# The score mask of an attention step is cut where its maximum is cut: three heads' mask and maximum, then the fourth head's

## The chip, the core and the metric

The kernel runs on one core of a Trainium2 chip. The metric is the time of one execution on the device, in microseconds; the time of a kernel is the median of several runs. The engines are named as in the profile: PE (TensorE matmul), PEld (TensorE weight load, which overlaps with PE), DVE (VectorE), ACT (ScalarE), POOL (GpSimd), SP (SyncE).

## What is computed

A transformer block of one sequence of 2048 tokens, 640 wide: a modulated layer norm, attention of 32 heads (20 wide) in a sliding window of 256 tokens, a residual, a second modulated layer norm and an MLP (1536 wide, tanh GELU). Cut to the attention:

```python
qkv = (x @ wqkv).reshape(B, S, 3, H, Dh)          # H = 32, Dh = 20, W = 256
scores = einsum("bhqd,bhkd->bhqk", q, k) * Dh ** -0.5
mask = (idx[:, None] - idx[None, :] >= 0) & (idx[:, None] - idx[None, :] < W)
scores = where(mask, scores, -1e9)
p = softmax(scores, axis=-1)
o = einsum("bhqk,bhkd->bhqd", p, v)
```

## The kernel before

All matmuls run in fp32 or split a factor into a high and a low part. The program has three parts in time: a prologue to about 50 us (layer norm, first projections), attention with the projections laid between, to about 540 us, and the output projection and the MLP after that, which run on PE almost without a gap.

**The attention steps.** The heads are taken four at a time (a quad), the tokens in two halves, and a half in eight blocks of 128 queries. That makes 2 x 8 x 8 = 128 items, one per step t of the loop near the end of the function. A step t works on two items at once. The first is the scores item t (the tile s): queries against the three blocks of 128 keys in the window, for four heads. Only the maximum of each row is wanted from it, and goes into the tile nm. The second is the item t - 11 (LAG), the tile e: the same scores once more, turned round and with the maximum already subtracted through two more rows of the operands. It goes through the exponential into the tile pt, and two steps later (PVLAG) pt is multiplied with v into the tile o.

**What a step issues, in order.** On PE `score_batch` issues the e and the s matmuls as one mixed batch; then come the o matmuls (`pv_stage`), then a share of the projection's matmuls (tile pp), set by tables of numbers (EXTRA, LEAST, and so on). On DVE: the mask of e (`e_mask`), the mask of s and the maximum (`s_max`), then whatever the plan has put into this step: layer norm statistics, residues of projections, sums of the modulation. On ACT the exponential, on POOL the rest of the masking of pt. The engines' queues keep this program order (class `Ordered`).

**The s tile and its banks.** From step 11 to 127 the four heads of s lie side by side, 384 columns each, in one fixed tile that is used anew in every step (`score_banks`). It has three PSUM banks of 512 columns: head slot 0 lies in bank 0, slot 1 in banks 0 and 1, slot 2 in banks 1 and 2, slot 3 in bank 2. A matmul that would cross a bank is cut there (`cuts`). The order of the pieces in the mixed batch is the table BOTH: three of e, then slot 1's piece in bank 1, slot 1's piece in bank 0, slot 3 (bank 2), and so on. In a few batches two of these change places. So slot 3 is mostly the third s matmul of a batch, and it is the first to touch bank 2.

**The maximum in two pieces.** In 84 of the steps from 11 on the maximum is taken in two instructions: slots 0 to 2 (CUT = 3), which lie in banks 0, 1 and 2, then slot 3, in bank 2. In 33 steps, those of the table WHOLE, one instruction takes all four. Every maximum is kept in the list `maxima` with the banks that it reads. In the next step `score_batch` tells the scheduler that a matmul does not depend on a maximum of other banks. So the matmuls in banks 0 and 1 may start after the first maximum, and those in bank 2 after the second.

**The mask of s.** Of the three key blocks only two need a maximum: the oldest block's columns that are inside the window are copied over the masked-out columns of the newest block. That is `copy_predicated` on the last 128 columns of each head, with the first 128 as data (or a large negative constant, negc, where the oldest block does not exist). Before the change this is one instruction for all four heads, 128x512, ahead of both maxima.

All engine calls go through the helper `go` of `OrderedEngine`, so in the profile each stands at line 116, and the tiles' names tell them apart.

Of the kernel before, what the change touches and what calls it, by code (L numbers as in the profile page):

```python
# [17 lines left out]
P = 128  # L18
# [103 lines left out]
def block_kernel(ctx: ExitStack, tc: tile.TileContext, x, wqkv, wo, w1, b1, w2, b2, c, crow, wmod, wcol, sel, outT):  # L122
    core = tc.nc
    nc = Ordered(tc)
# [30 lines left out]
    negc = const.tile([P, 1, 1], F32, name="negc")  # L155
    nc.vector.memset(negc, NEG)
    mask_t = const.tile([P, 3, P], F32, name="mask_t")
    masks = {}
# [375 lines left out]
    fixed, maxima = {}, []  # L534
# [11 lines left out]
    def width():  # L546
        return 384 if LAG <= now[0] < 2 * NQB * QUADS else 512
# [65 lines left out]

    def s_max(it, s, c0):

        data = negc.to_broadcast([P, 4, P]) if c0 else s[:, :, 0:P]
        nc.vector.copy_predicated(s[:, :, 2 * P : 384], masks["s"].to_broadcast([P, 4, P]), data)
        del maxima[:]
        n = width()
        for lo, hi in ((0, CUT), (CUT, 4)) if n == 384 and now[0] not in WHOLE else ((0, 4),):  # L620
            red = nc.vector.tensor_reduce(
                it["quad"]["nm"][:, lo:hi, it["key"][2]], s[:, lo:hi, max(c0, P) : 384], AX.X, ALU.max
            )
            if n == 384:
                maxima.append((red.ins, range(lo * n // 512, (hi * n - 1) // 512 + 1)))

    def m_rows(it):
        half, quad, _, _ = it["key"]
# [515 lines left out]
    def lay_units(room):  # L1144
        used, act = collections.Counter(), collections.Counter()
        for t in asides:
            used[t] += 0.5
        t, turns, where = 0, {}, []
        for i, (key, c2) in enumerate(seq):
            fast = i < FAST  # L1150
            acc = (lambda i=i: pools["o"].tile([P, CHUNK], F32, tag="o", name=f"ppo{i}")) if fast and i % 2 else None
            mms, ev = unit(*key, c2, nc.vector if i in LOV else gp, acc)
            if key[0] and 2 + c2 in turns:
                t = max(t, turns[2 + c2] + 1)
            t0, left = t, list(mms)
            pieces = []
            while left:
                have = room * (t + 1 - FAST) - sum(used[j] for j in range(FAST, t + 1))
                n = len(left) if fast else min(len(left), max(LEAST, int(have + 0.5) + EXTRA.get(t, 0)))
                if len(left) - n < 3 and n < MOST:  # L1160
                    n = len(left)
                pieces.append((t, left[:n]))
                used[t] += n
                left = left[n:]
                t += 1
            where.append((i, key, c2, pieces, ev))
            if key[1] == 2:
                used[t] += V_COST
            if not key[0] and not [1 for k, c in seq[i + 1 :] if not k[0] and c == c2]:

                at = max(t, turns[2] + 5) if c2 else t
                for kt in range(KT):
                    used[at + kt] += X_COST
                turns[2 + c2] = at + KT + (1 if c2 else 2)
        return t, where, turns

    lo, hi = 4.0, 16.0
    for _ in range(30):
        room = (lo + hi) / 2
        lo, hi = (lo, room) if lay_units(room)[0] <= LAST else (room, hi)  # L1180
    _, where, turns = lay_units(hi)
    ready_w = [(seq[0][0], 0)]
    for i, key, c2, pieces, ev in where:
        t0, t1 = pieces[0][0], pieces[-1][0]
        for t, mms in pieces:
            cut = max(len(mms) - 3, 3)
# [73 lines left out]
    for (mms, (copy, turn)), lo, hi in zip(units, LATE_AT[3::2], LATE_AT[4::2]):  # L1260
        spread(plan, [step(1, go) for go in mms], lo, hi)
        hi = max(hi, TOMID + 0.5)
# [38 lines left out]
    n = len(s_items)  # L1301
# [6 lines left out]
    for t in range(n + LAG + PVLAG + 4):  # L1308
# [31 lines left out]
        if si:  # L1340
            s_max(si, *got)
# [47 lines left out]
    for ch in range(nch):  # L1389
        yhi, ylo = ([y[:, kt] for kt in range(KT)] for y in yT[ch % 2])  # L1390
        ts = slice(ch * CHUNK, (ch + 1) * CHUNK)
        lo, hi = (LO0, 9) if ch == 0 else (4 * ch + 5, 4 * ch + 9)
# [100 lines left out]
```

## Time and profile before

| | us |
|---|---|
| median of 3 runs | 977.62 |
| lowest and highest run | 977.16, 978.79 |
| the profiled execution | 978.3 |
| its span in the profile | 976.6 |
| granted clock of TensorE, mean | 0.998 |

The span goes from the first to the last instruction of the profiled execution. The rows of the profile read: engine, operation, output tile <- input tiles, shape, number; then busy time and mean duration in ns; then the engine's idle time just ahead of them and what ended it. Rows of the timeline read: start in us, duration in us, engine, line, operation; neighbouring instructions of one kind stand in one row, with the number behind x and the shape of the first. Rows of the waits read: who waited, for whom, us in total, number of times, the longest. Rows of windows read: stretch, its length, busy time of PE, PEld, DVE, ACT and POOL, the granted clock, the share of the DMA engines, GB/s.

### The profile page before, as it was taken

The numbers are of one execution on the slowest core, as the hardware profiler recorded it, in microseconds if no ns is written. First come the engines' busy times: TensorE is split into PE (matmuls) and PEld (weight loads), VectorE is DVE, ScalarE is ACT, GpSimd is POOL, SyncE is SP. The second block draws the span as 40 slices with busy tenths as digits, with TensorE's granted clock in tenths as the row PEclk, the third lists the DMA queues.
The fourth block names the chain that finished last, engine by engine and source line by source line (L and its number), as shares of the span: only waits on it lengthen the run. The fifth ranks groups of instructions, "written<-read, shape, count | busy, mean of one in ns | idle before, by whom it ended". The sixth has DMA issues, their size and how long they took to land.

```text
span 976.6 us, 20093 instructions
## 1 busy us (share of the span) xinstructions
PE 947.7 (97%) x7789; PEld 752.6 (77%) x7789; DVE 592.9 (61%) x999; ACT 442.4 (45%) x777; POOL 485.8 (50%) x673
## 2 busy tenths in 40 slices
PE   8899999999999999999898999999999999999998
PEld 8677777777777777777677787888888888888886
DVE  6564977978776786767888556563534444342112
ACT  3724555666644545555545654434333243333222
POOL 4423555677864364553646844654554454332121
PEclk9999999999999999999999999999999999999999
DMA  8366778756778459854852245444423342114113
GB/s 307 99 207 199 243 226 260 224 170 168 220 231 236 121 174 283 241 155 120 224 161 76 81 137 161 127 130 138 138 57 103 115 144 85 54 57 145 54 43 119
DMA packets 98974, 152.17 MB, mean 156 GB/s; under 512 B 8864, under 2 KB 42112, under 8 KB 98880
## 3 DMA queue, kind: packets, MB, share of 16 engines
q1 hardware_dynamic: 89664, 142.50, 48.2%
q10 hardware_dynamic: 9216, 8.39, 2.7%
q8 instruction: 62, 1.02, 0.4%
q14 instruction: 32, 0.26, 0.1%
HBM read 98.51 MB, written 51.58 MB: 154 GB/s over the span
## 4 chain that ended last, share of the span: by engine, by line
PE 82%; DVE 7%; ACT 4%; POOL 2%; DMA 2%; issue 2%; SPq 1%; DVEq 0%; POOLq 0%; ACTq 0%
PE pp L116 17%; PE out L116 16%; PE h L116 16%; PE e L116 8%; PE o L116 7%; PE wo L116 7%; PE s L116 4%; ACT pt L116 3%; DVE e L116 2%; PE ppo L116 2%; DVE nm L116 1%; PE yt L116 1%; PE pv L116 1%; PE xt L116 1%; DMA wc<-in_wcol 1%
## 5 line engine op out<-in xcount | busy, mean ns | idle before, releaser
L116 POOL TENSOR_SCALAR_AFFINE_SELECT pt<-pt 128x512 f32<-128x512 f32 x192 | 127.7, 665 | 131.8 <-ACT pt L116 119.4
L116 ACT ACTIVATE pt<-e 128x1024 f32<-128x1024 f32 (+1 forms) x120 | 133.7, 1115 | 67.2 <-DVE e L116 63.8
L116 DVE TENSOR_REDUCE nm<-s 128x1 f32<-128x256 f32 (+5 forms) x212 | 158.0, 779 | 4.4
L116 POOL TENSOR_TENSOR w2lo<-w2r,w2hi 128x640 fp32r<-128x640 f32 x48 | 78.7, 1639 | 160.2 <-ACT w2hi L116 160.2
L116 DVE CAST ghi<-g 128x512 fp32r<-128x512 f32 x48 | 28.1, 585 | 155.7 <-ACT g L116 155.7
L116 PE MATMUL e<-qbuf,kbuf 62*128 62x128 f32 (+2 forms) x773 | 112.8, 330 | 9.1 <-ACT pt L116 7.6
L116 PEld LDWEIGHTS e<-qbuf,kbuf 62*128 62x128 f32 x773 | 81.2, 186 | 48.5 <-ACT pt L116 23.2
L116 PE MATMUL pp<-hhi,w_hi 128*128 128x512 f32 x265 | 113.4, 428 | 0.2 <-ACT pf L116 0.2
L116 PE MATMUL s<-kbuf,qbuf 60*128 60x384 f32 (+2 forms) x728 | 106.6, 303 | 4.0 <-DVE nm L116 1.6
L116 PE MATMUL pp<-hlo,w_hi 128*128 128x512 f32 x265 | 108.1, 408 | 1.3 <-POOL hlo L116 1.3
L116 DVE COPY_PREDICATED e<-mask_t,e 128x512 f32<-128x512 uint32 x96 | 66.6, 694 | 66.2 <-PE e L116 62.6
L116 PE MATMUL pp<-hhi,w_lo 128*128 128x512 f32 x265 | 106.8, 403 | 0.0
L116 PEld LDWEIGHTS s<-kbuf,qbuf 60*128 60x128 f32 x728 | 89.8, 187 | 14.0 <-DVE nm L116 6.1
L116 PE MATMUL o<-pt,vbuf 128*32 128x128 f32 x2688 | 99.6, 277 | 0.7 <-ACT xT L116 0.7
L116 PE MATMUL out<-ghi,w2hi 128*128 128x512 f32 x240 | 95.5, 398 | 0.5 <-ACT g L116 0.5
L116 PE MATMUL out<-glo,w2hi 128*128 128x512 f32 x240 | 94.0, 391 | 0.0
L116 PE MATMUL out<-ghi,w2lo 128*128 128x512 f32 x240 | 93.9, 391 | 0.0
L116 POOL TENSOR_TENSOR w_lo<-wraw,w_hi 128x128 fp32r<-128x128 f32 x171 | 76.0, 475 | 32.6 <-ACT w_hi L116 32.6
L116 PE MATMUL h<-yhi,w1hi 128*128 128x512 f32 x220 | 87.8, 399 | 0.0
L116 PE MATMUL h<-ylo,w1hi 128*128 128x512 f32 x220 | 86.2, 392 | 0.0
L116 PE MATMUL h<-yhi,w1lo 128*128 128x512 f32 x220 | 86.0, 391 | 0.0
L116 DVE COPY_PREDICATED s<-mask_t,s 128x512 f32<-128x512 uint32 x112 | 77.1, 689 | 11.8 <-PE s L116 11.5
(179 smaller groups left out, 1839.0 us busy)
## 6 DMA issues: line engine op xcount, KB each, us to landing
w2r<-in_w SPq DMA_DIRECT2D x48, 320.0 KB
qbuf<-q_scr SPq DMA_DIRECT2D x60, 240.0 KB
wraw<-in_wqkv SPq DMA_DIRECT2D x36, 320.0 KB
kbuf<-k_scr SPq DMA_DIRECT2D x44, 240.0 KB
q_scr<-stage SPq DMA_DIRECT2D x20, 512.0 KB
k_scr<-stage SPq DMA_DIRECT2D x20, 512.0 KB
o_scr<-oT ACTq DMA_DIRECT2D x64, 128.0 KB
wm<-in_wmod SPq DMA_DIRECT2D x20, 320.0 KB
```

The lines of the kernel that those rows point to most:

```text
L116: return self.tc.keep_in_program_order(op(*args, **kw))
```

## The change

In the 84 steps in which the maximum is taken in two pieces, the mask is too, cut at the same head, and each piece of the mask stands directly ahead of its maximum. In all other steps nothing changes. The pieces of the mask enter the list `maxima` with the banks of their slots, so that the next step's matmuls in banks 0 and 1 do not depend on the fourth head's mask either.

```diff
     def s_max(it, s, c0):
 
-        data = negc.to_broadcast([P, 4, P]) if c0 else s[:, :, 0:P]
-        nc.vector.copy_predicated(s[:, :, 2 * P : 384], masks["s"].to_broadcast([P, 4, P]), data)
         del maxima[:]
         n = width()
         for lo, hi in ((0, CUT), (CUT, 4)) if n == 384 and now[0] not in WHOLE else ((0, 4),):
+            data = negc.to_broadcast([P, hi - lo, P]) if c0 else s[:, lo:hi, 0:P]
+            cut = nc.vector.copy_predicated(
+                s[:, lo:hi, 2 * P : 384], masks["s"].to_broadcast([P, hi - lo, P]), data
+            )
             red = nc.vector.tensor_reduce(
                 it["quad"]["nm"][:, lo:hi, it["key"][2]], s[:, lo:hi, max(c0, P) : 384], AX.X, ALU.max
             )
             if n == 384:
-                maxima.append((red.ins, range(lo * n // 512, (hi * n - 1) // 512 + 1)))
+                banks = range(lo * n // 512, (hi * n - 1) // 512 + 1)
+                maxima.extend((op.ins, banks) for op in (cut, red))
```

How the instructions stand on DVE in step 94 (the one that the prediction follows in the timeline), before, with what each waits for; e is the tile of the turned scores, s the scores, nm the maxima:

```order
L116 COPY_PREDICATED e_2_3_5439<-mask_t,e_2_3_5439 128x4x128 [waits PE_49,Activation_49]
L116 COPY_PREDICATED s_1_3_995<-mask_t,s_1_3_995 128x4x128 [waits DVE_49,PE_49]
L116 TENSOR_REDUCE nm_3_5105<-s_1_3_995 128x3 [waits DVE_49]
L116 TENSOR_REDUCE nm_3_5105<-s_1_3_995 128x1
L116 COPY_PREDICATED e_2_4_5490<-mask_t,e_2_4_5490 128x4x128 [waits PE_49,Activation_49]
```

and in the changed kernel, the same step on DVE:

```order
L116 COPY_PREDICATED e_2_3_5499<-mask_t,e_2_3_5499 128x4x128 [waits PE_49,Activation_49]
L116 COPY_PREDICATED s_1_3_995<-mask_t,s_1_3_995 128x3x128 [waits DVE_49,PE_49]
L116 TENSOR_REDUCE nm_3_5160<-s_1_3_995 128x3 [waits DVE_49]
L116 COPY_PREDICATED s_1_3_995<-mask_t,s_1_3_995 128x128 [waits DVE_49]
L116 TENSOR_REDUCE nm_3_5160<-s_1_3_995 128x1 [waits DVE_49]
L116 COPY_PREDICATED e_2_4_5551<-mask_t,e_2_4_5551 128x4x128 [waits PE_49,Activation_49]
```

The mask of s has become two instructions, and the second stands between the two maxima. DVE_49 is the semaphore that DVE's own instructions count up. The fourth head's mask waits until the first maximum is done, and the fourth head's maximum until that mask is done; before, the second maximum had no wait of its own. The first mask still waits for the last matmul of the batch that it needs.

On PE the order is the same in both kernels. The batch that follows these maxima, in the changed kernel:

```order
L116 MATMUL e_2_4_5551<-qbuf_100,kbuf_103 128x256 [waits Activation_49]
L116 MATMUL e_2_4_5551<-qbuf_100,kbuf_103 128x384 x2
L116 MATMUL s_1_3_995<-kbuf_104,qbuf_101 128x256 [waits DVE_49]
L116 MATMUL s_1_3_995<-kbuf_104,qbuf_101 128x128
L116 MATMUL s_1_3_995<-kbuf_104,qbuf_101 128x384 [waits DVE_49]
```

The first s matmul (slot 1, bank 1) waits for the maximum of three heads, the third (slot 3, bank 2, 128x384) for the maximum of the fourth. In this kernel as before, each of the two is held only by its own maximum; what moved is what stands ahead of these maxima on DVE. ACT, POOL and the DMA queues have the same rows in both kernels.

## The prediction

> **What bounds the kernel now.** I read the page first (busy times), then the stretch in which attention runs, then the waits of TensorE and VectorE in that stretch, and at last single steps in the timeline.
>
> ```profile
> span 976.6 us, 20093 instructions
> PE 947.7 (97%) x7789; PEld 752.6 (77%) x7789; DVE 592.9 (61%) x999; ACT 442.4 (45%) x777; POOL 485.8 (50%) x673
> ```
> ```profile
> 100.00:540.00 440.00, 426.85 (x4879) 319.53 (x4878) 348.12 (x516) 239.36 (x446) 256.96 (x400) 1.00 0.66 195
> 540.00:977.00 437.00, 429.64 (x2406) 359.49 (x2404) 186.65 (x339) 157.98 (x254) 192.69 (x210) 1.00 0.34 105
> ```
> The two window rows give busy time of PE, PEld, DVE, ACT and POOL, then the granted clock. The change touches only 100 to 540 us, where the score tile is 384 wide. There PE is busy 427 of 440 us and DVE 348: PE sets the pace, but DVE is close behind, and full speed was granted throughout (1.00). A microsecond by which PE is held up there moves the end by as much, since behind it PE is just as full.
>
> Who holds PE up in this stretch:
>
> ```profile
> PEld s L116 <- DVE nm L116: 6.1, 15, 1.2
> ```
> The weight loads of the next scores wait for the maxima (nm), 6.1 us in all. This row counts only idle time; how close the other steps are is seen in one ordinary step (94):
>
> ```profile
> 408.45 0.70 DVE L116 COPY_PREDICATED e<-mask_t,e 128x512 f32<-128x512 uint32 x1 [0.77 <-PE e L116]
> 409.06 0.69 DVE L116 COPY_PREDICATED s<-mask_t,s 128x512 f32<-128x512 uint32 x1
> 409.78 1.29 DVE L116 TENSOR_REDUCE nm<-s 128x3 f32<-128x768 f32 x2
> 411.84 0.70 DVE L116 COPY_PREDICATED e<-mask_t,e 128x512 f32<-128x512 uint32 x1 [0.77 <-PE e L116]
> ```
> ```profile
> 411.12 0.18 PEld L116 LDWEIGHTS s<-kbuf,qbuf 60*128 60x128 f32 x1
> ```
> The two maxima end at 409.78 + 1.29 = 411.07. At 411.12, 0.05 later, the load for the fourth head starts, the one that writes bank 2. What is left of the batch takes until 411.84, where the mask of e starts. So the step is a ring: mask of e, mask of s, two maxima, fourth head on PE, rest of e, mask of e. It takes 3.39 us (411.84 - 408.45), and whatever lengthens DVE's part between the mask of s and the second maximum lengthens it by as much.
>
> Of the 84 steps with two maxima I set the end of the second against the start of the fourth head's load. In 35 the load starts 0.05 us after, as here: it is the second maximum that it waits for. The first and the last of the 35:
>
> ```profile
> 111.04 0.42 DVE L116 TENSOR_REDUCE nm<-s 128x1 f32<-128x256 f32 x1
> ...
> 522.95 0.42 DVE L116 TENSOR_REDUCE nm<-s 128x1 f32<-128x256 f32 x1
> ```
> ```profile
> 111.51 0.18 PEld L116 LDWEIGHTS s<-kbuf,qbuf 60*128 60x128 f32 x1
> ...
> 523.42 0.18 PEld L116 LDWEIGHTS s<-kbuf,qbuf 60*128 60x128 f32 x1
> ```
> In 25 more the load comes less than 0.31 us later than that; their slacks lie between 0.01 and 0.30 us and add up to 3.75 us. The first of these is a maximum that ends at 118.64, with a load 0.24 later, a slack of 0.19:
>
> ```profile
> 118.36 0.28 DVE L116 TENSOR_REDUCE nm<-s 128x1 f32<-128x128 f32 x1
> ```
> ```profile
> 118.88 0.18 PEld L116 LDWEIGHTS s<-kbuf,qbuf 60*128 60x128 f32 x1
> ```
> The last is that of 534.07 (slack 0.26). In the other 24 steps the slack is larger.
>
> **The change, part by part.** PE, ACT, POOL and the DMA queues keep their order; DVE gets 84 instructions more. Durations, from the groups of DVE in the same stretch (mean ns behind the busy time):
>
> ```profile
> L116 DVE TENSOR_REDUCE nm<-s 128x3 f32<-128x768 f32 x81 | 77.7, 959 | 2.8
> L116 DVE COPY_PREDICATED s<-mask_t,s 128x512 f32<-128x512 uint32 x104 | 71.6, 688 | 2.8 <-PE s L116 2.6
> ...
> L116 DVE TENSOR_REDUCE nm<-s 128x4 f32<-128x1024 f32 x30 | 36.8, 1226 | 1.0
> ...
> L116 DVE TENSOR_REDUCE nm<-s 128x1 f32<-128x256 f32 x81 | 33.6, 415 | 0.0
> ...
> L116 DVE COPY_PREDICATED_SCALAR s<-mask_t,negc 128x512 f32 x12 | 8.9, 744 | 0.0
> ```
> *Length of the masks.* From 256 to 1024 columns a maximum grows by (1226 - 415) / 768 = 1.056 ns a column, between 768 and 1024 by 1.04: about 0.133 us for one head's 128 columns, and a fixed part near 0.15. No mask of another width stands in the trace. Three heads' mask is then 0.69 - 0.13 = 0.56; the fourth's is 0.69 - 0.40 = 0.29. Its bounds are 0.13 (columns alone) and 0.69 (width without effect). I take 0.29, since the maximum of the same 128 columns above took 0.28.
>
> *Hand-overs.* In step 94 the mask of s starts 0.09 before the mask of e ends (409.06 against 409.15): its waits were over long before. The first maximum waits for the mask and starts 0.03 after its end (409.78 against 409.75). The second waits for nothing new: the pair takes 1.29 and its parts 0.96 + 0.415, so it starts 0.085 before the first ends. A wait on the instruction just ahead thus costs about 0.12 us. In the new order both the fourth head's mask and its maximum have such a wait.
>
> *The sum for one step,* from the start of the first mask. Before: first maximum ends at 0.72 + 0.96 = 1.68, second at 0.72 + 1.29 = 2.01. After: mask 0.56, maximum from 0.59 to 1.55, mask from 1.58 to 1.87, maximum from 1.90 to 2.32. The first maximum ends 0.13 earlier, the second 0.31 later. I call these 0.31 D. With the bounds of the short mask D is 0.15 to 0.71; the rows near it make that 0.25 to 0.37, down if one of the two waits costs half as much, up by the 0.056 by which the form with a constant (744) exceeds the other (688).
>
> Against one row a rule can be laid: one maximum over four heads takes 1.226, two without a wait between them 1.29, so one more instruction alone costs 0.064. The Trainium skill, in Vector Engine (DVE) Microarchitecture Reference, section 5.2 Measured stream behaviour on trn2, gives about 75 ns per instruction beside 1.0417 ns a column, after queue overlap; the rows agree, and it speaks against splitting. By that alone the 35 steps would lose 2.6 us, an estimate from its figure; I go by the rows with a wait.
>
> *What of it lies on the path.* The earlier end of the first maximum frees banks 0 and 1 sooner, but the fourth head stands third among the s matmuls of the batch, and PE takes its queue in order: what starts sooner waits at the fourth head. I count this gain as nothing. If I am wrong it is 0.13 in each of the 16 steps whose first load of s starts 0.05 after the first maximum's end, 2.1 us; the first and the last of the 16:
>
> ```profile
> 110.17 0.96 DVE L116 TENSOR_REDUCE nm<-s 128x3 f32<-128x768 f32 x1
> ...
> 509.06 0.96 DVE L116 TENSOR_REDUCE nm<-s 128x3 f32<-128x768 f32 x1
> ```
> ```profile
> 111.18 0.18 PEld L116 LDWEIGHTS s<-kbuf,qbuf 60*128 60x128 f32 x1
> ...
> 510.07 0.18 PEld L116 LDWEIGHTS s<-kbuf,qbuf 60*128 60x128 f32 x1
> ```
> The later second maximum costs 35 x 0.31 = 10.9, and 25 x 0.31 - 3.75 = 4.0 in the near ones: 14.9. Counting slack to the start of the matmul and not of its load, since PE often still has a matmul under way, gives 11.7. I take the middle, 13.3.
>
> Behind the waiting instruction on DVE stands the next mask of e or other work. In most steps DVE is idle ahead of that mask:
>
> ```profile
> DVE e L116 <- PE e L116: 68.3, 71, 2.4
> ```
> That cover is missing where statistics or residues fill the gap, as here:
>
> ```profile
> 221.99 1.29 DVE L116 TENSOR_REDUCE nm<-s 128x3 f32<-128x768 f32 x2
> 223.20 0.88 DVE L116 BATCH_NORM_STATS2 st<-xt 128x6 f32<-128x320 f32 x2
> 224.18 0.21 DVE L116 BATCH_NORM_AGGREGATE mv<-st 128x2 f32<-128x12 f32 x1
> 224.30 0.68 DVE L116 COPY_PREDICATED e<-mask_t,e 128x512 f32<-128x512 uint32 x1
> ```
> There the mask of e starts late, with it the exponential and the next e matmuls. This step passes its 0.31 on to the next, and the two behind it have no idle time here either, so nearly 0.9 us gather. For two or three such places I put 2 us (0 to 3), an estimate. Against that, PE's waits for work that does not hang on the mask shrink when PE comes later:
>
> ```profile
> PEld pm L116 <- ACT oT L116: 2.2, 3, 1.4
> PEld e L116 <- ACT w_hi L116: 1.8, 5, 0.4
> PEld e L116 <- ACT oT L116: 1.4, 4, 0.4
> ```
> Of these 5.4 us I take off a quarter, 1.3 (0 to 3). The sum: 13.3 + 2 - 1.3 = **14 us**.
>
> The profiled execution took 978.3 us (span 976.6), 0.7 over the median of the runs, 977.62. So 978.3 becomes 992.3, and the median **991.6**.
>
> **Rivals.**
> 1. *The waits are free.* If handing over costs nothing extra, D falls by 2 x 0.12 to 0.07, and the 35 steps lose 2.5, the near ones 0.2: 980.3. The 0.03 against -0.085 in the step above speaks against it. The Trainium skill has this rule, in VectorE: DVE Perf Modes, section The DRAIN you can't avoid: a semaphore between chained instructions costs nothing extra; here the trace does not agree. Chance 0.06.
> 2. *Faster: the first maximum decides.* Banks 0 and 1 come free 0.13 sooner in the 16 steps: 975.5. It needs a second maximum that ends no later than now, so a short mask with all its hand-overs within the 0.13 that the first mask gives back; I have 0.44 (0.29 + 2 x 0.03 + 0.085). For it only that the rows hold no mask of 128 columns. Chance 0.03.
> 3. *DVE becomes the bound.* DVE gains 84 x 0.31 = 26 us on 348 in a stretch of 440. If every step pays in full: 1003.6. For it the stretch at 222 us; against it the 71 waits of DVE for PE. Chance 0.08.
> 4. *It is hidden:* PE's records overlap, so a late load might go into time that PE does not need: 977.6. The ring of step 94 speaks against it. Chance 0.03.
>
> **How the numbers follow.** The forecast has 0.80. Its low end is D = 0.25 with the slack to matmul starts, 8.75, plus 1 for DVE's backlog and less 3: 6.5, so 984. Its high end is D = 0.37 by loads, 18.6, plus 3: 21.6, so 999. The range 984 to 999 leaves 0.2 outside. About 0.2% (2 us) is what a measurement tells from no change. Faster: rival 2, 0.03. Same: rival 4 and, since 2.7 us is near that bound, two thirds of rival 1, 0.07. Slower: the rest, 0.90.
>
> **What would show it.** In the profile after, on DVE a mask of 128x384 near 0.56 and one of 128x128 near 0.29, each 84 times; the second maximum 2.3 us after the start of the first mask and the first 1.55; DVE some 25 us busier. The wait of PEld s for nm well above 6.1 us, with many more cases, and the ring of step 94 near 3.7 us. Everything after 540 us should keep its length. I am wrong in the price if the second maximum ends within 2.1, wrong in the path if it ends at 2.3 and PE does not wait more.

## The result and the profile after

The changed kernel takes 994.76 us (median of 4 runs, 993.24 to 995.16) against 977.39 (4 runs, 976.78 to 978.79): the ratio is 1.0165, with a 95% interval of 1.0152 to 1.0177. It is 17.4 us slower; 14 were forecast. First the page of the changed kernel, its span and busy times, then the row of the stretch from 100 us to where the attention steps end (557 us here, 540 before):

```profile
span 993.5 us, 20178 instructions
PE 959.4 (97%) x7789; PEld 758.9 (76%) x7789; DVE 613.0 (62%) x1083; ACT 442.0 (44%) x777; POOL 486.4 (49%) x673
```
```profile
100.00:557.00 457.00, 437.47 (x4877) 324.30 (x4876) 367.99 (x600) 238.66 (x445) 257.23 (x400) 0.99 0.64 188
```
The stretch is 17 us longer (457 against 440). PE's busy time in it grew by 10.6 us, its idle time by the other 6.4. The groups of matmuls on PE in these stretches, e and s, before:

```profile
L116 PE MATMUL e<-qbuf,kbuf 62*128 62x128 f32 (+1 forms) x715 | 105.5, 329 | 7.0 <-ACT pt L116 6.3
L116 PE MATMUL s<-kbuf,qbuf 60*128 60x256 f32 (+2 forms) x678 | 99.5, 299 | 1.7 <-DVE nm L116 1.6
```
and in the changed kernel:

```profile
L116 PE MATMUL e<-qbuf,kbuf 62*128 62x128 f32 (+1 forms) x715 | 112.3, 330 | 7.4 <-ACT pt L116 6.7
L116 PE MATMUL s<-kbuf,qbuf 60*128 60x256 f32 (+2 forms) x678 | 109.5, 303 | 7.7 <-DVE nm L116 6.6
```
Six of the 6.4 us of idle time stand ahead of the s matmuls (7.7 against 1.7). The same number of matmuls of e and s fill 16.8 us more though a single one is only 1 to 4 ns longer: where they are held up, they follow each other with less overlap. So busy time on PE hides a part of the waiting. The granted clock, 0.99 here and 1.00 before, is not the cause: the run without needless waits (below) has 0.99 in its stretch too and takes as long as before the change:

```profile
100.00:540.00 440.00, 426.91 (x4880) 319.72 (x4878) 344.62 (x600) 239.65 (x446) 258.60 (x400) 0.99 0.66 195
```
The part behind the steps kept its length: from the end of the last maximum to the end of the program it is 438.9 us before and 438.4 after.

Step 94 again, on DVE in the changed kernel:

```profile
420.30 0.69 DVE L116 COPY_PREDICATED e<-mask_t,e 128x512 f32<-128x512 uint32 x1 [0.77 <-PE e L116]
420.90 0.56 DVE L116 COPY_PREDICATED s<-mask_t,s 128x384 f32<-128x384 uint32 x1
421.49 0.96 DVE L116 TENSOR_REDUCE nm<-s 128x3 f32<-128x768 f32 x1
422.49 0.29 DVE L116 COPY_PREDICATED s<-mask_t,s 128x128 f32<-128x128 uint32 x1
422.81 0.42 DVE L116 TENSOR_REDUCE nm<-s 128x1 f32<-128x256 f32 x1
424.01 0.70 DVE L116 COPY_PREDICATED e<-mask_t,e 128x512 f32<-128x512 uint32 x1 [0.77 <-PE e L116]
```
and the weight loads of the batch that follows these maxima:

```profile
422.58 0.37 PEld L116 LDWEIGHTS s<-kbuf,qbuf 60*128 60x128 f32 x2
423.29 0.18 PEld L116 LDWEIGHTS s<-kbuf,qbuf 60*128 60x128 f32 x1 [0.35 <-DVE nm L116]
```
From the start of the first mask the first maximum ends after 1.55 us (421.49 + 0.96 - 420.90) and the second after 2.34 (to three places of the trace; 422.81 + 0.42 - 420.90 = 2.33). Before it was 1.68 and 2.01. Only the first load of s comes earlier here, 1.67 after the start of the first mask (422.58 - 420.90, to three places) instead of 1.73, and the first s matmul starts at 1.85 as before. The third load then stands idle for 0.35 until the second maximum is done. The idle time of DVE ahead of the mask of e is 0.77 as before: the ring is the same, only longer. It takes 3.71 us (424.01 - 420.30) instead of 3.39.

The groups of masks and maxima, and the waits of the weight loads for them:

```profile
L116 DVE TENSOR_REDUCE nm<-s 128x3 f32<-128x768 f32 x81 | 77.7, 959 | 2.8
...
L116 DVE COPY_PREDICATED s<-mask_t,s 128x384 f32<-128x384 uint32 x75 | 41.6, 554 | 2.3 <-PE s L116 2.3
...
L116 DVE TENSOR_REDUCE nm<-s 128x1 f32<-128x256 f32 x81 | 34.4, 424 | 2.8
...
L116 DVE COPY_PREDICATED s<-mask_t,s 128x128 f32<-128x128 uint32 x75 | 22.2, 297 | 2.6
```
```profile
PEld s L116 <- DVE nm L116: 15.4, 43, 1.1
PEld pm L116 <- ACT oT L116: 2.2, 3, 1.4
...
PEld e L116 <- ACT w_hi L116: 1.4, 4, 0.4
```
The masks took 0.554 and 0.297 us. The 2.6 and 2.8 us of idle time ahead of the fourth head's mask and maximum are the two hand-overs, 0.03 each time (the nine masks with a constant and the three narrower maxima stand in rows of their own). The loads of s now wait 15.4 us in 43 cases, where it was 6.1 in 15.

**Where the 17 us arise.** The mask of e starts a step in both kernels, so from one such row to the next the difference between the two timelines tells what a step lost. The row of the first cut step (13), ahead of its masks, and of step 127, in the changed kernel:

```profile
105.16 0.70 DVE L116 COPY_PREDICATED e<-mask_t,e 128x512 f32<-128x512 uint32 x1 [0.43 <-PE e L116]
```
```profile
552.55 0.70 DVE L116 COPY_PREDICATED e<-mask_t,e 128x512 f32<-128x512 uint32 x1 [0.38 <-PE e L116]
```
and before, with the same two rows:

```profile
104.96 0.70 DVE L116 COPY_PREDICATED e<-mask_t,e 128x512 f32<-128x512 uint32 x1 [0.43 <-PE e L116]
```
```profile
535.11 0.70 DVE L116 COPY_PREDICATED e<-mask_t,e 128x512 f32<-128x512 uint32 x1 [0.65 <-PE e L116]
```
The lag grows from 0.20 to 17.44 us. Added up by the step whose maxima stand ahead, from the mask of s of one step to that of the next: 10.6 us behind the 35 steps in which the fourth head's load had waited already, 4.8 behind the 25 near ones, 0.4 behind the 24 with more slack, and 1.4 behind the steps that were not cut. Of these 1.4, step 55 has 0.36, which step 54 handed on to it, and step 121 has 0.85. There the granted clock of this profiled execution stood at 0.50 for 3.4 us (527.3 to 530.7 us), where before it was 1.00; whether the change brings that on is not shown.

### The profile page after: what moved, and what is told of

It reads as the page before. It is cut to its first block, busy times and chain, and to the rows that moved or that the text cites. A ratio compares the mean times of both kernels' runs of the same rounds, so it can differ in the third digit from the quotient of the medians.

```text
span 993.5 us, 20178 instructions
## 1 busy us (share of the span) xinstructions
PE 959.4 (97%) x7789; PEld 758.9 (76%) x7789; DVE 613.0 (62%) x1083; ACT 442.0 (44%) x777; POOL 486.4 (49%) x673
## 4 chain that ended last, share of the span: by engine, by line
PE 75%; DVE 13%; issue 5%; ACT 2%; DMA 2%; POOL 2%; SPq 1%; DVEq 0%; POOLq 0%; ACTq 0%
PE out L116 16%; PE h L116 16%; PE pp L116 14%; PE e L116 6%; PE wo L116 6%; PE o L116 6%; DVE nm L116 5%; PE s L116 4%; DVE s L116 3%; DVE e L116 2%; PE ppo L116 2%; ACT pt L116 1%; PE yt L116 1%; DVE st L116 1%; PE xt L116 1%
## 5 line engine op out<-in xcount | busy, mean ns | idle before, releaser
L116 DVE TENSOR_REDUCE nm<-s 128x1 f32<-128x256 f32 (+5 forms) x212 | 165.8, 782 | 7.3
L116 PE MATMUL e<-qbuf,kbuf 62*128 62x128 f32 (+2 forms) x773 | 119.6, 331 | 9.5 <-ACT pt L116 8.0
L116 PE MATMUL s<-kbuf,qbuf 60*128 60x384 f32 (+2 forms) x728 | 116.5, 306 | 10.0 <-DVE nm L116 6.6
L116 PEld LDWEIGHTS e<-qbuf,kbuf 62*128 62x128 f32 x773 | 83.8, 185 | 48.9 <-ACT pt L116 24.1
L116 PEld LDWEIGHTS s<-kbuf,qbuf 60*128 60x128 f32 x728 | 95.2, 186 | 25.4 <-DVE nm L116 15.4
L116 DVE COPY_PREDICATED s<-mask_t,s 128x384 f32<-128x384 uint32 (+2 forms) x187 | 89.3, 478 | 14.8 <-PE s L116 12.1
L116 ACT COPY oT<-o 128x128 f32<-128x128 f32 x128 | 33.8, 264 | 122.3 <-PE o L116 118.3
```

The source lines that it names most:

```text
L116: return self.tc.keep_in_program_order(op(*args, **kw))
```

## The experiments

Two theories stood against each other. *The ring:* the 0.33 us by which the second maximum comes later are paid where PE's fourth head waits for it, and nowhere else. *DVE's load:* DVE has more to do, and every added instruction costs the same wherever it stands. A third question was the price itself: an instruction more, or the waits between the instructions. The kernel before was measured again beside each group of runs, and its time stands with each.

### The cut in some steps only

```diff
+APART = [14, 17, 20, 21, 25, ...]          # the 35 tight steps; in the other run, the 24 slack ones
+        apart = now[0] in APART
+        if not apart:
+            copy_predicated(s[:, :, 2 * P : 384], ...)     # one mask
         for lo, hi in pieces:
+            if apart: copy_predicated(s[:, lo:hi, 2 * P : 384], ...)
             tensor_reduce(...)
```

> The mask is cut only in the 35 steps in which the fourth head's load waited for the second maximum in the trace of before; the other 49 split steps keep one mask. Ring theory (the delay of the second maximum is paid where PE waits for it): 35 x 0.33 = 11.6 us, so 987 to 991. Rival, DVE's load (every added instruction costs the same wherever it stands): 35/84 of 17.4 = 7.2 us, so 984 to 985. Rival, no path at all: 977.

> The mask is cut only in the 24 steps whose slack behind the second maximum was over 0.31 us. Ring theory: the 0.33 us is covered, 0 to 2 us (the few of these steps in which DVE is not idle ahead of the mask of e), so 977 to 979.5. Rival, DVE's load: 24/84 of 17.4 = 5.0 us, so 982.

With the 35 tight steps alone the kernel takes 990.52 us against 978.30, ratio 1.0128 (1.0106 to 1.0150), 12.2 us. With the 24 slack steps alone it takes 978.54 against 978.30, ratio 1.0005 (0.9996 to 1.0014), nothing that can be measured. The weight loads' waits in the first and in the second (the helper stands at line 117 in them):

```profile
PEld s L117 <- DVE nm L117: 15.4, 42, 1.1
```
```profile
PEld s L117 <- DVE nm L117: 6.4, 16, 1.2
```
The first run has all of the waits that the full change has, the second hardly more than before. DVE's load would have given 7.2 and 5.0 us. This is the ring, and the slack read from the trace of before tells which steps pay. What the near steps add, 4.8 us by the timelines, stands in no row of waits: these are 15.4 in the full change too, and PE's idle time is 19.4 us of 452 in the first run and 19.5 of 457 in the full change. It is time in which PE counts as busy, and only the timelines show it.

### The same delay without the cut, and the same load behind it

The mask stays whole. A maximum over a constant tile, whose result nobody uses, is added in the 84 steps, once between the two maxima and once behind them.

```diff
 for lo, hi in pieces:
+    if lo: tensor_reduce(fill_t, mask_t[:, 0:2], AX.X, ALU.max)      # load_between
     red = tensor_reduce(nm[:, lo:hi, ...], s[:, lo:hi, ...], AX.X, ALU.max)
+if split: tensor_reduce(fill_t, mask_t[:, 0:2], AX.X, ALU.max)       # load_behind
```

> The mask stays one instruction; in the 84 split steps a maximum over a constant tile in SBUF (256 columns, result unused) is put between the two maxima. It delays the second maximum by about 0.3 us and leaves the first where it was. Ring theory: 35 x 0.30 and the near steps, 14.3 us, plus 2 of backlog: 990 to 996. Rival, that the cut mask itself is to blame (its waits, or a mask in PSUM holding up PE): 977 to 980.

> The same added maximum over a constant tile, but behind the second maximum: DVE has as much more to do as in the run with it between, and the second maximum ends where it did. Ring theory: only the steps in which DVE is not idle ahead of the mask of e pay, 1 to 5 us, so 978.5 to 982.5. Rival, DVE's load: as much as between, 990 to 996.

Step 94 on DVE with the added instruction between:

```profile
420.13 0.69 DVE L116 COPY_PREDICATED s<-mask_t,s 128x512 f32<-128x512 uint32 x1
420.86 0.96 DVE L116 TENSOR_REDUCE nm<-s 128x3 f32<-128x768 f32 x1
421.73 0.41 DVE L116 TENSOR_REDUCE fill_t<-mask_t 128x1 f32<-128x256 f32 x1
422.06 0.42 DVE L116 TENSOR_REDUCE nm<-s 128x1 f32<-128x256 f32 x1
```
and with it behind:

```profile
411.75 1.29 DVE L116 TENSOR_REDUCE nm<-s 128x3 f32<-128x768 f32 x2
412.96 0.41 DVE L116 TENSOR_REDUCE fill_t<-mask_t 128x1 f32<-128x256 f32 x1
413.82 0.70 DVE L116 COPY_PREDICATED e<-mask_t,e 128x512 f32<-128x512 uint32 x1 [0.45 <-PE e L116]
```
Between, it delays the second maximum to 2.34 after the start of the mask (to the trace's three places), as the change does, and the kernel takes 996.75 us against 978.30: ratio 1.0190 (1.0175 to 1.0205). Behind, it only eats into DVE's idle time ahead of the mask of e (0.45 left of 0.77), and the kernel takes 982.97: ratio 1.0055 (1.0036 to 1.0075). DVE's load is the same in both. The rows of the timelines tell them further apart than the times do: up to step 127 the lag is 16.0 us with it between and 2.7 with it behind. The rest, 2.9 us between and 1.6 behind, arose after the steps, where neither kernel is changed (last section); by it both times lie a little above what was expected. A cut mask is not needed for the loss; a late second maximum is enough. Nor does the earlier first maximum help: between, it ends at 1.68 as before, in the change at 1.55, and the 35 tight steps lose 10.7 and 10.6 us.

### Fewer waits, the same instructions

Three kernels keep both masks and both maxima and change only their order or what waits for what. In the first, both masks go ahead of both maxima. The second keeps the order of the change, but the fourth head's mask no longer waits for the first maximum, whose columns it doesn't touch. The third has the masks first and no wait between instructions on different heads.

```diff
# masks_first: for piece: copy_predicated; then for piece: tensor_reduce
# one_wait: the change, and
+            if before is not None: tc.declare_no_dep(cut.ins, before.ins, reason="other heads")
# no_waits: masks_first, and
+        tc.declare_no_dep(cuts_[1].ins, cuts_[0].ins, reason="other heads")
+            tc.declare_no_dep(red.ins, other.ins, reason="other heads")      # the other piece's mask
```

> Both masks, then both maxima. As built, the fourth head's mask still waits for the first mask and the first maximum for the fourth head's mask, but the second maximum waits for nothing new: one wait less than in the change. By the hand-over price of 0.12 us the second maximum ends 0.19 later than before (and the first 0.19 later): 8.1 us direct and 1 to 2 of backlog, so 985 to 988. Rival, that waits are free and the instruction alone costs: no difference from the change, 993 to 996.

> The change with its order, but the fourth head's mask no longer waits for the first maximum (they touch other heads' columns, so there is no hazard); the fourth head's maximum still waits for its mask. The second maximum ends 0.20 later than before instead of 0.33. By the hand-over price of 0.12 us: 8.6 us direct, 1 to 2 of backlog, 985.5 to 988.5. Rival, waits are free: as the change, 993 to 996.

> Both masks, then both maxima, and no wait between instructions on other heads' columns: the fourth head's mask does not wait for the first mask, the first maximum only for the first mask, which by then is done, the second only for the fourth head's mask. The extra instruction costs 0.07 and stands in for the one wait that was there (0.12): both maxima end 0.04 earlier than before. By the hand-over price: 35 x 0.04 = 1.4 us less than before, 975 to 977. Rival, waits are free and an instruction costs its share: 3 to 17 us more than before.

Step 94 with one wait taken out, on DVE:

```profile
416.89 0.56 DVE L116 COPY_PREDICATED s<-mask_t,s 128x384 f32<-128x384 uint32 x1
417.48 0.96 DVE L116 TENSOR_REDUCE nm<-s 128x3 f32<-128x768 f32 x1
418.36 0.29 DVE L116 COPY_PREDICATED s<-mask_t,s 128x128 f32<-128x128 uint32 x1
418.68 0.43 DVE L116 TENSOR_REDUCE nm<-s 128x1 f32<-128x256 f32 x1
```
The fourth head's mask starts 0.08 before the first maximum ends (418.36 against 418.44); with the wait it started 0.04 after (422.49 against 422.45). That is the 0.12 per wait, here read from one pair of instructions. The second maximum ends 2.21 after the start, not 2.34 (to the trace's three places). The kernel takes 986.97 us against 977.87, ratio 1.0093 (1.0080 to 1.0106). With the masks first it is 986.83, ratio 1.0098 (1.0085 to 1.0111), and the second maximum ends at 2.21 there too. So one wait less in 84 steps is worth about 8 us of the 17.

Step 94 without needless waits:

```profile
407.79 0.75 DVE L116 COPY_PREDICATED s<-mask_t,s 128x384 f32<-128x384 uint32 x2
408.45 1.28 DVE L116 TENSOR_REDUCE nm<-s 128x3 f32<-128x768 f32 x2
```
The first maximum starts 0.09 before the second mask ends (408.45 against 408.54; its own mask, 0.56 long, is done by then), and the second before the first is done; it ends 1.94 after the start, 0.07 earlier than before the change, with an instruction more. The kernel takes 977.19 us against 977.87: ratio 0.9994 (0.9986 to 1.0003), not to be told from no change. The whole loss of the change is gone, but the expected gain of 1.4 us (975 to 977) is not shown by the times. In the timeline 1.0 us is gained behind the 35 tight steps and 0.5 behind the slack ones, and 1.4 is lost behind the near ones. These 1.4 stand in steps 114 and 115 alone. From the mask of s of step 114 to that of step 116, before and in this run:

```profile
486.80:494.80 8.00, 6.29 (x83) 5.38 (x83) 6.58 (x11) 5.15 (x9) 0.78 (x1) 0.79 0.22 54
```
```profile
485.30:494.80 9.50, 7.73 (x83) 6.55 (x83) 6.58 (x13) 5.11 (x9) 0.82 (x1) 0.64 0.27 75
```
The granted clock was 0.64 there in this profiled execution and 0.79 in that of before. The control below (the kernel before with two maxima in every step), whose own steps 114 and 115 are those of before, lost 1.5 us in them, at 0.64 too. The run below with both masks first in every step, whose instructions in these two steps are those of this run, took 7.4 us for them at a clock of 1.00, where it is 7.9 before and 9.3 here. So the loss goes with the clock of an execution and not with the masks. It is one execution of each kernel, and so a hint at the gain and no proof.

### Another order on PE

The two pieces of s in bank 2 go last in the mixed batch.

```diff
-BOTH = ['0f', '0c', '0d', '1a', '1b', '1d', '0b', '1e', '0a', '0e', '1c', '1f']
+BOTH = ['0f', '0c', '0d', '1a', '1b', '0b', '0a', '0e', '1c', '1f', '1d', '1e']
```

> The change, and in the mixed batch the two pieces of s in bank 2 (the fourth head, and the third head's) go last; to be read against the same order without the change. Ring theory: the fourth head comes some 0.4 us later on PE, behind all of e, so most of the 0.33 is covered: 1 to 6 us more than the same order without the change. Rival, DVE's load: 15 to 18 us more.

> The kernel before, and in the mixed batch the two pieces of s in bank 2 go last; the other half of the pair with the change in that order, which took 991.9. Ring theory: the change costs 1 to 6 us in this order, so this one takes 986 to 991. Rival, DVE's load: 974 to 977, since the order would then cost nothing.

Without the change this order takes 988.68 us (ratio to before 1.0111, 1.0096 to 1.0125), with it 991.87 (1.0146, 1.0133 to 1.0159). Here the change costs 3.2 us by the medians; the two kernels were not measured side by side, but each against the kernel before. The loads' waits for the maxima, without the change and with it:

```profile
PEld s L116 <- DVE nm L116: 5.3, 13, 1.1
```
```profile
PEld s L116 <- DVE nm L116: 5.9, 15, 0.9
```
They grow by 0.6 us, where they grew by 9.3 in the order of before (and the loads wait 1.5 us for the masks of s, 1.8 in the changed kernel). With the fourth head further back in PE's queue most of the 0.33 us is covered, as the ring has it. The two profiled executions differ by only 0.1 us at the end of the last maximum, but they are no fair pair: in steps 114 and 115 the granted clock was 0.60 without the change and 1.00 with it, and the two steps took 9.6 and 7.5 us. The order itself costs 11 us, so it is no way to use the change; the cause of these 11 was not looked for.

### Both masks first, no needless waits, in every step

If two maxima without needless waits end no later than one, the table of the steps with one maximum has no use any more.

```diff
# all_split: no_waits, and        # before_all_split: the kernel before, and
-WHOLE = [11, 12, 23, 24, ...]
+WHOLE = []
```

> Both masks, then both maxima, without needless waits, in all 117 steps from 11 on (the table of the steps with one maximum is empty). In its own steps the earlier run showed the second maximum 1.945 after the start of the first mask and the first 1.615, where one mask and one maximum take 1.95. So in the 33 added steps bank 0 and 1 come free 0.33 earlier and nothing later: 8 or 9 of them have a load that waited for the one maximum, 1 to 2.5 us in all: 974 to 977. If DVE's load decided, it would be 0 to 2 us more than before.

> The kernel before with the table of the steps with one maximum empty: one mask, two maxima in all 117 steps. Control for the run above. There the second maximum ends 2.01 after the start of the mask instead of 1.95, the first 1.68: 0 to 2 us less than before, 976 to 978, if what the 33 steps gain is the earlier first maximum, and then the masks in two give the rest of the run above.

The second of the two is the control. It takes 978.62 us against 978.05, ratio 1.0008 (0.9998 to 1.0017): nothing gained, where 976 to 978 was expected. The first takes 976.70, ratio 0.9986 (0.9977 to 0.9995), 1.4 us faster than before the change and 18 faster than the changed kernel. Its loads wait 4.1 us for the maxima between 100 and 540 us, those of the run without needless waits 5.8 (before it was 6.1):

```profile
PEld s L116 <- DVE nm L116: 4.1, 10, 1.2
```
```profile
PEld s L116 <- DVE nm L116: 5.8, 13, 1.2
```
So the cut mask is of use when its pieces wait only for what they touch, as far as so small a gain can show it: its interval reaches to 0.05%.

## Why the prediction was right, point by point

*The ring and its price.* Right. Step 94 was forecast at near 3.7 us and took 3.71; the masks at 0.56 and 0.29 took 0.554 and 0.297; the first maximum ends at 1.55 as forecast. D, put at 0.31, came out as 0.33, since the fourth head's maximum grew from 415 to 424 ns and its mask was 7 ns longer.

*Nothing from the earlier first maximum.* Right: in seven of the 16 steps (14, 21, 35, 41, 77, 105 and 110) the first matmul of s starts 0.12 to 0.14 earlier after the mask, and then the fourth head holds the batch up; in step 94 and most of the others not even this matmul starts earlier. The run with an instruction between the maxima, in which the first maximum is not earlier, loses as much in the tight steps.

*The tight and the near steps.* The tight ones were put at 10.9 and lost 10.6, the near ones at 4.0 and lost 4.8. Together 15.4, close to the 14.9 of the count by weight loads. The step that failed is "I take the middle, 13.3": slack counted to the start of the matmul (11.7) was too kind, and the middle was 1.6 us too low against the load count alone. Single steps show which slack counts: steps 18, 99 and 58, with slacks of 0.03, 0.11 and 0.25 by the load, lost 0.28, 0.21 and 0.07. By the matmul's start it would have been 0.19, 0.10 and nothing. That the sum came so close is in part luck. With D at 0.33 the 35 tight steps would have lost 11.4, but two of them (35 and 110) lost nothing; and five near ones (32, 36, 44, 46 and 125) lost the full 0.32 to 0.35 in spite of their slack.

*What DVE hands on, and what PE saves elsewhere.* Forecast as 2 less 1.3. DVE's backlog is there: the place at 222 us is steps 44 to 46, put at nearly 0.9 us, and they lost 0.97. Four of the five near steps just named (all but 36) and the slack steps 34 and 45 lose about as much when the added instruction stands behind the second maximum, so it is DVE without idle time that they pay for. The 5.4 us of PE's other waits shrank by 0.7, to 2.2, 1.4 and 1.1. The steps outside the two groups show 1.8 together, and 0.85 of that is the step at half the clock. The forecast has no such term: it read "full speed was granted throughout" from a mean of 1.00, while in the execution of before, too, the clock stood at 0.50 for 3.4 us (490.4 to 493.8). So 2.1 of the 3 us between 14 and 17 come from the middle, the 0.02 in D and the near steps with a backlog, and 0.85 from the clock of one execution; some 0.2 is left. After 540 us everything kept its length, as said.

*DVE's busy time.* I expected 25 us more; it is 20.1 (613.0 against 592.9). Much of what a wait costs is not busy time: the hand-over leaves the engine idle, 2.6 and 2.8 us in the two rows above.

*The rivals.* Waits that cost nothing: fell, by two kernels with the same instructions as the change and one wait less, which were some 8 us faster. The first maximum decides: fell. DVE becomes the bound: fell as a rule, since the same load behind the second maximum lags 2.7 us up to step 127 instead of 16.0; it holds only for the few steps in which DVE has no idle time. It is hidden: fell.

## What to carry to other kernels

When an instruction is cut so that its consumer may start earlier, follow the last piece and not the first: in an in-order queue the earlier start is worth nothing if a later instruction of the same batch waits for a piece that now ends later. Price a cut by the extra instruction and by every wait on the instruction directly ahead (here 0.07 and 0.12 us), and look whether these waits guard anything; if pieces touch different data, let them not wait for each other, and issue producers first and consumers after them (here one wait less was worth 8 of the 17 us, both together all of them). To see who pays, take the slack between each release and the waiting weight load step by step. Its sum, 14.9 us, came near the 15.4 that these steps lost, with some errors that cancelled; the average load of the engine said nothing.

## What was not expected of the hardware

Adding the instruction on a constant tile lengthened the part of the program behind the steps as well, which is the same in all these kernels: 440.5 us with it behind and 441.8 between, in one profiled execution of each, against 438.1 to 439.3 in the other profiled executions. In both runs the MLP's matmuls on the high half took 403 ns on average, before the change 399. The row with it between:

```profile
L116 PE MATMUL h<-yhi,w1hi 128*128 128x512 f32 x220 | 88.8, 403 | 0.0
```
The two kernels differ from the others by a tile of 4 bytes per partition in a pool that lives through the whole program. Whether that is the cause was not tried and stays open.
